# A backward kernel for an S4 layer gated by a SwiGLU: stores of the gate gradients by quarters, and a pause in the parameter chunks

## The chip, the cores and the metric

The kernel runs on 1 core of one Trainium2 chip. The metric is the time of one execution on the device in microseconds (us). The engines are named as in the profile: PE is TensorE (matmul), DVE is VectorE, ACT is ScalarE, POOL is GpSimd, SP is SyncE. All engines run side by side, each through a queue of its own in a fixed order. DMAs are issued from such a queue too (here those of SP, POOL and ACT), so a transfer that stands behind a waiting instruction is issued late.

## The reference

With L = 2048 tokens, D = 576 channels, N = 128 states and F = 4608 hidden units, the forward pass is, cut to what matters:

```python
xn = layernorm(x)
s  = irfft(rfft(xn) * rfft(K)) + xn * Dskip      # K from A, B, C, log_dt: an S4 convolution along L
h  = silu(xn @ w1) * (xn @ w3)                   # SwiGLU: w1, w3 are D x F
g  = silu(h @ w2)                                # w2 is F x D
out = x + s * g
```

The kernel returns `out` (out_0) and, for a given `grad_out`, the gradients of x (out_1), of A, B and C (real and imaginary parts), log_dt (out_8), Dskip, w1 (out_10), w3 (out_11) and w2 (out_12). Inputs and outputs are bfloat16.

## The kernel before

**Stages.** The forward part (layernorm, the convolution as a transform by matmuls, the SwiGLU) fills about the first 800 us. It leaves the gate products in device memory: `G_dram` holds xn @ w1 and `U_dram` xn @ w3, in NG = 18 groups of FG = 256 hidden units. Everything after that is in `backward`, which lays three streams of work over each other:

1. The **gradient pass**, 18 groups, to 1705 us in the profiled execution. `phase6_load` brings a group's G and U on POOL's queue into `gg_n` and `h_n` (L1192, L1193, 1 MB each); ACT makes Silu into `gu_n` (L1197) and then Derivative_silu in place (L1199); DVE multiplies both with U (L1201, L1202). There are two sets of these three buffers, so group gi+1 is loaded and prepared while group gi is worked on, and its load must wait until the buffers of group gi-1 are free. `phase6_group` then makes the gradient of the hidden units. In four steps s, each for two token tiles in both halves j of the sequence, PE computes `ph` from `goT` and `w2T` (L1224), ACT copies it to `gh` (L1227), and DVE multiplies `gh` into `gu_n` and `gg_n` (L1230). After the second and the fourth step PE computes half of the gradient of w2 (`phase6_grad2`, matmuls L1251, eviction `gw2` L1255, store to out_12 on POOL L1256). After all four steps POOL stores `gu_n` and `gg_n` as GU and GG in device memory, `GU_dram` and `GG_dram`, in two halves of 512 KB each (L1233 to L1236). Last, `phase6_grad13` computes the gradients of w3 and w1 (matmuls `pgw` L1270, evictions `gw` L1272).

2. The **parameter chunks** of the convolution, 36 of them (`ssm_bwd_params`). For each, `param_load` issues on SP two small loads `gz` (L1007), a transposing DMA `qT` from `Q_dram`, and a load `pz` (L1012); three chunks' buffers exist, and loads run two chunks ahead. `param_chunk` does 16 matmuls into `et_ps` in four quads (L1025), and after each quad DVE makes two products `pr_q` (L1032) and a sum into `S_all` (L1036). When all chunks are done, `phase5_final` closes this work in five pieces of up to 128 channels: PE transposes `S_all` (L1055), ACT copies it to `ST`, DVE does some 45 small operations per piece with the rates loaded by `load_rates`, and each piece's results `gout` go out through three buffers on SP and ACT. A last small store, `gl_bf` to out_8, is issued on SP (L1118, L1120).

3. The **second pass** (`phase6_inputs`), from 1705 us on: the gradient of xn for 16 tiles of 128 tokens. Each tile needs `ggc` and `guc`, transposing DMAs of GG and GU on SP (`nat_transpose`, L1177), then 144 matmuls `px` of 128x288 (L1314) against the transposed weights. `finish` adds the convolution's part (`gx`, DVE L1324), and `ln_bwd_tile` goes back through the layernorm and stores out_1. `ggc`, `guc` and the two `px` each have two buffers, so a tile may begin when the tile two before it has let go of them. The 36 blocks of the transposed weights come in four parts (blocks 0 to 15, 16 to 22, 23 to 29, 30 to 35), brought by SP as well: `wTA` in good time during the gradient pass; part 1 and half of part 2 into the gradient pass's buffers once they are free (the profile calls them `gg_n`, `h_n` and `gu_n` there too); the other half of part 2 (`wTB`) and part 3 (`wT`) when their space is free. Because the weights come one after another, the first two tiles are computed part by part, both tiles in each part.

**The order.** A scheduler builds each engine's queue when the program is built. `self.at(us)` gives the instructions that follow a due time, which serves as their priority: of those that are ready in the scheduler's model, the one due first goes first. On the chip each queue then runs in the order so fixed. The call is `backward(700, TG=36, TQ=75, TC=14, TX=18)`: in due times, the gradient pass starts at T0 = 700 with a group each 36; the chunks start at T1 = 1000, one each 14; the second pass starts at T2 = 700 + 18 x 36 = 1348, a tile each 18. Due times are not device times, only their order counts.

Of the kernel before, what the change touches and what calls it, by code (L numbers as in the profile page):

```python
# [60 lines left out]
class K:  # L61
# [837 lines left out]
            for g in range(4):  # L899
                self.conv_bwd_quarter(g, kp, zp, ps, T0 + g * TQ, TQ)  # L900

    def ssm_bwd_params(self, T0, TC, S_all, ps):
        cfg = self.cfg
        D, LT = cfg.D, cfg.LT
        with self.tc.tile_pool(name="g_k", bufs=1, side="right") as gkp, self.tc.tile_pool(name="g_q", bufs=2, side="right") as qp:
            gz = []
            for i in range(3):
                z = gkp.tile([P, 2, 2, 2, 16, LT], BF16, name=f"gz{i}")
                self.nc.gpsimd.memset(z[:], 0.0)
                gz.append(z)  # L910
            NCH = D // 16
            AHEAD = 2
            q = []
            for ch in range(NCH + AHEAD):
                if ch < NCH:
                    self.at(T0 + TC * (ch - AHEAD))
                    q.append(self.param_load(ch, gz[ch % 3], qp))
                if ch >= AHEAD:
                    self.at(T0 + TC * (ch - AHEAD))
                    self.param_chunk(ch - AHEAD, q.pop(0), S_all, qp, ps)  # L920

    def conv_bwd_quarter(self, g, kp, zp, ps, T0, TQ):
# [202 lines left out]
    def backward(self, T0, TG, TQ, TC, TX, gctx, mats):  # L1125
        nc, cfg = self.nc, self.cfg
        D, L, LT, F, FT = cfg.D, cfg.L, cfg.LT, cfg.F, cfg.FT
        self.GG_dram = self.dram.tile([LT, P, F], BF16, name="GG_dram")
        self.GU_dram = self.dram.tile([LT, P, F], BF16, name="GU_dram")
        self.GXN_dram = self.dram.tile([P, LT, D], FP32, name="GXN_dram")  # L1130
        NG = F // self.FG
        T2 = T0 + TG * NG
        FA = 16
        pool = self.tc.tile_pool
        PS = bass.MemoryType.PSUM
        with ExitStack() as out:
            ffn = ExitStack()
            wp = ffn.enter_context(pool(name="e_w", bufs=2))
            inp = [self.in0, ffn.enter_context(pool(name="e_in1", bufs=1))]
            elp = ffn.enter_context(pool(name="e_el", bufs=3))  # L1140
            gwp = ffn.enter_context(pool(name="e_gw", bufs=2))
            ps_h = ffn.enter_context(pool(name="e_ps_h", bufs=3, space=PS))
            ps_gw = ffn.enter_context(pool(name="e_ps_gw", bufs=2, space=PS))
            ps = out.enter_context(pool(name="b_ps", bufs=3, space=PS, side="right"))
            self.ssm_bwd_conv(T0, TQ, ps)
            mats.close()
            fix = out.enter_context(pool(name="b_fix", bufs=1, side="right"))
            S_all = fix.tile([P, 4, D], FP32, name="S_all")
            wA = out.enter_context(pool(name="x_wA", bufs=1, side="right"))
            wT = [[self.load_wT1(wA.tile([P, FA, D], BF16, name=f"wTA{k}"), k, 0, FA, T2 - 190 + 75 * k, 15) for k in range(2)]]  # L1150
            T1 = T0 + 4 * TQ
            self.ssm_bwd_params(T1, TC, S_all, ps)
            self.at(T1 + TC * D // 16)
            self.phase5_final(out, fix, S_all, ps, T1 + TC * D // 16, TX)
            cur = self.phase6_load(0, T0 - TG, TG, wp, inp)
            for gi in range(NG):
                nxt = self.phase6_load(gi + 1, T0 + TG * gi, TG, wp, inp) if gi + 1 < NG else None
                self.at(T0 + TG * gi)
                self.phase6_group(gi, cur, elp, gwp, ps_h, ps_gw)
                cur = nxt  # L1160
            ffn.close()
            gctx.close()
            self.phase6_inputs(T2, TX, FA, wT)
# [15 lines left out]
    def phase6_load(self, gi, T, TG, wp, inp):  # L1179
        nc, cfg = self.nc, self.cfg  # L1180
        self.at(T)
        D, DT, LT = cfg.D, cfg.DT, cfg.LT
        aps = self.aps
        FG = self.FG
        assert 2 * (DT * P - D) == P
        w2T = wp.tile([P, DT, FG], BF16, name="w2T")
        self.nat_transpose(w2T[:], self.W2_dram[gi * FG:(gi + 1) * FG, :])
        inp = inp[gi % 2]
        gg = inp.tile([P, LT, FG], BF16, name="gg_n")
        hn = inp.tile([P, LT, FG], BF16, name="h_n")  # L1190
        gu = inp.tile([P, LT, FG], BF16, name="gu_n")
        nc.gpsimd.dma_start(out=gg[:], in_=self.G_dram[gi])  # L1192
        nc.gpsimd.dma_start(out=hn[:], in_=self.U_dram[gi])  # L1193
        quarters = [slice(s * LT // 4, (s + 1) * LT // 4) for s in range(4)]
        self.at(T + 0.4 * TG)
        for sl in quarters:
            nc.scalar.activation(out=gu[:, sl, :], in_=gg[:, sl, :], func=ACT.Silu)  # L1197
        for sl in quarters:
            nc.scalar.activation(out=gg[:, sl, :], in_=gg[:, sl, :], func=ACT.Derivative_silu)  # L1199
        for sl in quarters:  # L1200
            nc.vector.tensor_tensor(out=gg[:, sl, :], in0=gg[:, sl, :], in1=hn[:, sl, :], op=ALU.mult)  # L1201
            nc.vector.tensor_tensor(out=hn[:, sl, :], in0=gu[:, sl, :], in1=hn[:, sl, :], op=ALU.mult)  # L1202
        return w2T, hn, gg, gu

    def phase6_group(self, gi, tiles, elp, gwp, ps_h, ps_gw):
        nc, cfg = self.nc, self.cfg
        D, LT, FG = cfg.D, cfg.LT, self.FG
        nfull = D // P
        rem = D - nfull * P
        LH = LT // 2  # L1210
        w2T, hn, gg, gu = tiles
        pair = lambda t_: t_[:].rearrange("p (j t) f -> p j t f", j=2)
        for s in range(LH // 2):
            gh = elp.tile([P, 2, 2, FG], BF16, name="gh6")
            ph = [ps_h.tile([P, 2, FG], FP32, name="ph") for _ in range(2)]
            for k in range(2):
                t = s * 2 + k
                for j in range(2):
                    tt = j * LH + t
                    rs = slice(j * rem, (j + 1) * rem)  # L1220
                    steps = [(self.goT[:, c, tt * P:(tt + 1) * P], w2T[:, c, :]) for c in range(nfull)]
                    steps.insert(nfull * (1 - j), (self.goTt[rs, t * P:(t + 1) * P], w2T[rs, nfull, :]))
                    for n, (lw, rh) in enumerate(steps):
                        nc.tensor.matmul(ph[j][:, k, :], lhsT=lw, rhs=rh, start=(n == 0),  # L1224
                                         stop=(n == nfull))
            for j in range(2):
                nc.scalar.copy(out=gh[:, j], in_=ph[j][:])  # L1227
            sl = slice(s * 2, s * 2 + 2)
            for t_ in (gu, gg):
                nc.vector.tensor_tensor(out=pair(t_)[:, :, sl], in0=gh[:], in1=pair(t_)[:, :, sl], op=ALU.mult)  # L1230
            if s % 2 == 1:
                self.phase6_grad2(gi, s // 2, hn, gwp, ps_gw)
        for (dst, t_) in ((self.GU_dram, gu), (self.GG_dram, gg)):  # L1233
            for j in range(2):
                ts = slice(j * LH, (j + 1) * LH)
                nc.gpsimd.dma_start(out=dst[ts, :, gi * FG:(gi + 1) * FG].rearrange("t p f -> p t f"), in_=t_[:, ts, :])  # L1236
        self.phase6_grad13(gi, gg, gu, gwp, ps_gw)

    def phase6_grad2(self, gi, fl, hn, gwp, ps_gw):
# [239 lines left out]
```

## Time and profile before

| | us |
|---|---|
| five runs | 2050.97, 2033.35, 2070.73, 2043.77, 2058.24 |
| their median | 2050.97 |
| the profiled execution | 2074.11 |
| span in its profile, first to last instruction | 2072.3 |

| engine | busy us | share of the span |
|---|---|---|
| PE (16144 instructions) | 1788.5 | 86% |
| DVE | 1505.3 | 73% |
| ACT | 968.4 | 47% |
| POOL | 468.2 | 23% |

The core's DMA engines moved 421.27 MB, 203 GB/s on average. The mean granted clock of PE was 0.95 of full speed. L12 is line 12 of the kernel's file. In a row of the timeline the columns are: start, duration, engine (SPq is SP's queue, where DMAs are issued), line, operation, output<-input, shapes, and in brackets the idle time before it with what ended it.

### The profile page before, as it was taken

How to read it: one execution, taken by the hardware profiler on the slowest of the kernel's cores; microseconds unless marked ns; L12 is line 12 of the kernel's file. 1: busy time of each engine (PE TensorE's matmuls, PEld its weight loads, DVE VectorE, ACT ScalarE, POOL GpSimd, SP SyncE). 2: the span in 40 equal slices, each digit the busy share in tenths (PEclk: the TensorE clock that was granted, in tenths of full speed). 3: DMA queues.
4: the chain of work that ended last, by engine and by line, in shares of the span. 5: the costliest groups of instructions: out<-in, count | busy, mean ns of one | idle time of the engine just before them, and what ended most of it. 6: DMA issues, size and time to landing. Idle time of an engine off the chain costs nothing. (4 is left out here: it accounts for less than half of the span.)

```text
span 2072.3 us, 40290 instructions
## 1 busy us (share of the span) xinstructions
PE 1788.5 (86%) x16144; PEld 1250.7 (60%) x16214; DVE 1505.3 (73%) x2616; ACT 968.4 (47%) x1733; POOL 468.2 (23%) x610
## 2 busy tenths in 40 slices
PE   2888988889898799989898999876996994899997
PEld 1443333335453577777777777755775773677785
DVE  7459999998783465478696878666895985677851
ACT  1968888886455311474747565333453420000000
POOL 6016666661123011111111111211211210000000
PEclk9899999999999899999999999988998997899998
DMA  6688788877579988546463635999878799999894
GB/s 177 238 278 294 265 279 276 283 259 253 177 260 191 213 202 190 170 134 190 130 196 117 205 126 160 202 224 172 241 204 152 209 234 180 219 230 191 171 176 62
DMA packets 550828, 421.27 MB, mean 203 GB/s; under 512 B 414320, under 2 KB 481072, under 8 KB 546032
## 3 DMA queue, kind: packets, MB, share of 16 engines
q1 hardware_dynamic: 488096, 254.56, 52.0%
q0 software_dynamic: 37904, 147.48, 22.6%
q10 hardware_dynamic: 24640, 16.65, 3.0%
q8 instruction: 127, 2.08, 0.4%
q14 instruction: 61, 0.50, 0.1%
HBM read 135.96 MB, written 196.27 MB: 160 GB/s over the span
## 5 line engine op out<-in xcount | busy, mean ns | idle before, releaser
L1270 PEld LDWEIGHTS <-xn_bf 128*128 128x128 bf16 x2304 | 225.1, 98 | 30.1 <-issue 2.6
L1032 DVE TENSOR_TENSOR pr_q<-et_ps,pz 128x512 f32<-128x512 f32 x288 | 186.1, 684 | 68.4 <-DMA pz<-PZ_dram 32.3
L768 PEld LDWEIGHTS <-xnT 128*128 128x128 bf16 x1152 | 101.7, 98 | 172.6 <-issue 76.5
L1224 PE MATMUL ph<-w2T,goT 128*128 128x256 bf16 x1152 | 179.2, 287 | 3.4 <-DVE e L840 2.0
L1036 DVE TENSOR_REDUCE S_all<-pr_q 128x16 f32<-128x1024 f32 x144 | 175.0, 1216 | 2.2
L1251 PE MATMUL pgw<-go_o,h_n 128*128 128x288 bf16 x1152 | 163.8, 292 | 0.0
L768 PE MATMUL pu<-wmB_w,xnT 128*128 128x512 bf16 x565 | 152.9, 386 | 5.0 <-ACT u_t L778 3.7
L768 PE MATMUL pg<-wmB_w,xnT 128*128 128x512 bf16 x523 | 145.6, 382 | 9.1 <-issue 5.6
L499 POOL COPY pz_k<-p_k 128x256 bf16<-128x256 bf16 x144 | 140.2, 1016 | 46.5 <-issue 37.4
L1272 ACT CAST gw<-pgw 128x256 bf16<-128x256 f32 x144 | 54.6, 380 | 204.0 <-PE pgw L1270 202.7
L831 PE MATMUL po<-w2g,hc 128*128 128x288 bf16 x1152 | 147.5, 291 | 1.3 <-ACT u_t L778 1.3
L1363 ACT ACTIVATE t<-gx 128x576 f32<-128x576 f32 x16 | 10.9, 684 | 282.1 <-DVE gx L1324 282.1
L1314 PEld LDWEIGHTS <-guc 128*128 128x128 bf16 x1152 | 114.4, 100 | 44.8 <-DMA guc<-GU_dram 14.9
L1314 PEld LDWEIGHTS <-ggc 128*128 128x128 bf16 x1152 | 114.5, 100 | 39.1 <-DMA ggc<-GG_dram 9.4
L1230 DVE TENSOR_TENSOR gu_n<-gh,gu_n 128x1024 bf16<-128x1024 bf16 x72 | 49.4, 686 | 120.8 <-ACT gh L1227 120.8
L1270 PE MATMUL pgw<-gu_n,xn_bf 128*128 128x256 bf16 x1152 | 132.8, 272 | 1.5 <-ACT gw L1255 1.1
L831 PEld LDWEIGHTS <-hc 128*128 128x128 bf16 x1152 | 113.2, 99 | 32.5 <-issue 1.7
L1270 PE MATMUL pgw<-gg_n,xn_bf 128*128 128x256 bf16 x1152 | 130.8, 274 | 0.0
L1025 PE MATMUL et_ps<-gz,qT 128*128 128x128 bf16 x576 | 53.9, 228 | 89.0 <-DMA qT<-Q_dram 53.0
L1224 PEld LDWEIGHTS <-goT 128*128 128x128 bf16 x1152 | 103.2, 102 | 45.5 <-issue 14.2
L1251 PEld LDWEIGHTS <-h_n 128*128 128x128 bf16 x1152 | 112.7, 100 | 28.7
L1314 PE MATMUL px<-wTA,guc 128*128 128x288 bf16 x512 | 109.5, 297 | 13.1 <-DMA guc<-GU_dram 13.1
(321 smaller groups left out, 4232.3 us busy)
## 6 DMA issues: line engine op xcount, KB each, us to landing
G_dram<-g_t POOLq DMA_DIRECT2D x72, 256.0 KB, 3.9
U_dram<-u_t POOLq DMA_DIRECT2D x72, 256.0 KB, 3.3
H_dram<-h_t SPq DMA_DIRECT2D x72, 256.0 KB, 3.2
Q_dram<-q_k SPq DMA_DIRECT2D x36, 512.0 KB, 3.5
gg_n<-G_dram POOLq DMA_DIRECT2D x18, 1024.0 KB, 5.6
h_n<-U_dram POOLq DMA_DIRECT2D x18, 1024.0 KB, 8.9
GU_dram<-gu_n POOLq DMA_DIRECT2D x36, 512.0 KB, 6.3
GG_dram<-gg_n POOLq DMA_DIRECT2D x36, 512.0 KB, 8.5
```

The costliest lines, as they stand in the source:

```text
L499: nc.gpsimd.tensor_copy(out=pz[:, g, h, 1:3], in_=pv[:, g, h])
L768: nc.tensor.matmul(pt[:], lhsT=xnT[:, c, ts], rhs=wm[w][:, c, :], start=(c == 0 and not first), stop=(c == nfull - 1 and first))
L831: nc.tensor.matmul(po_[:, pi_, 0:pw], lhsT=hc[:, fi, :], rhs=w2[fi][:, po:po + pw], start=(fi == 0), stop=(fi == FT - 1))
L1025: nc.tensor.matmul(T[h][:, :, dd].rearrange("p r k (f t) -> p r (k f) t", f=2), lhsT=qT[:, dl, :], rhs=gK[:, :, :, :, dl, :].rearrange("p ...
L1032: nc.vector.tensor_tensor(out=pr[:, r].rearrange("p k m a -> p m k a"), in0=T[h][:, r][:, None].to_broadcast([P, 2, 4, 2, AV]), in1=pz[:, ...
L1036: nc.vector.tensor_reduce(out=S_all[:, :, d0:d0 + 4].rearrange("p (s k) d -> p k s d", k=2), in_=pr[:].rearrange("p r k (s d) a -> p k s d ...
L1224: nc.tensor.matmul(ph[j][:, k, :], lhsT=lw, rhs=rh, start=(n == 0), stop=(n == nfull))
L1230: nc.vector.tensor_tensor(out=pair(t_)[:, :, sl], in0=gh[:], in1=pair(t_)[:, :, sl], op=ALU.mult)
L1251: nc.tensor.matmul(pgw[pi_][:, 0:pw], lhsT=hn[:, tt, fl * P:(fl + 1) * P], rhs=go_o[:, tt, po:po + pw], start=(tt == 0), stop=(tt == LT - 1))
L1270: nc.tensor.matmul(pw_[:, 0:FG], lhsT=self.xn_bf[:, tt, c * P:(c + 1) * P], rhs=nat[:, tt, :], start=(tt == 0), stop=(tt == LT - 1))
L1272: nc.scalar.copy(out=gw[:, c, :], in_=pw_[:, 0:FG])
L1314: nc.tensor.matmul(px[pi_][:, 0:pw], lhsT=act[:, fi, :], rhs=wT[p][ai][:, fi - f0, po:po + pw], start=(fi == 0 and ai == 0), stop=(fi == F ...
```

## The change

Three edits. First, in `phase6_group` the stores of GU and GG go inside the loop over s: after the second and the fourth step, the token tiles finished so far are stored, two halves j of each array, before the w2 gradient of that step. That makes eight stores of 256 KB per group where there were four of 512 KB. Second, in `phase6_load` the due time of Silu and what follows goes from 0.4 to 0.45 of a group's 36. Third, in `ssm_bwd_params` a chunk whose due time lies after T2 - 30 = 1318 gets 40 more; with 1000 + 14c that is chunk 23 and all after it. The due times of `phase5_final` are not changed.

```diff
-    def ssm_bwd_params(self, T0, TC, S_all, ps):
+    def ssm_bwd_params(self, T0, TC, T2, S_all, ps):
...
             NCH = D // 16
             AHEAD = 2
             q = []
+            when = lambda c: T0 + TC * c + (40 if T0 + TC * c > T2 - 30 else 0)
             for ch in range(NCH + AHEAD):
                 if ch < NCH:
-                    self.at(T0 + TC * (ch - AHEAD))
+                    self.at(when(ch - AHEAD))
                     q.append(self.param_load(ch, gz[ch % 3], qp))
                 if ch >= AHEAD:
-                    self.at(T0 + TC * (ch - AHEAD))
+                    self.at(when(ch - AHEAD))
                     self.param_chunk(ch - AHEAD, q.pop(0), S_all, qp, ps)
...
-            self.ssm_bwd_params(T1, TC, S_all, ps)
+            self.ssm_bwd_params(T1, TC, T2, S_all, ps)
...
         quarters = [slice(s * LT // 4, (s + 1) * LT // 4) for s in range(4)]
-        self.at(T + 0.4 * TG)
+        self.at(T + 0.45 * TG)
...
             if s % 2 == 1:
+                for (dst, t_) in ((self.GU_dram, gu), (self.GG_dram, gg)):
+                    for j in range(2):
+                        ts = slice(j * LH + 2 * s - 2, j * LH + 2 * s + 2)
+                        nc.gpsimd.dma_start(out=dst[ts, :, gi * FG:(gi + 1) * FG].rearrange("t p f -> p t f"),
+                                            in_=t_[:, ts, :])
                 self.phase6_grad2(gi, s // 2, hn, gwp, ps_gw)
-        for (dst, t_) in ((self.GU_dram, gu), (self.GG_dram, gg)):
-            for j in range(2):
-                ts = slice(j * LH, (j + 1) * LH)
-                nc.gpsimd.dma_start(out=dst[ts, :, gi * FG:(gi + 1) * FG].rearrange("t p f -> p t f"), in_=t_[:, ts, :])
         self.phase6_grad13(gi, gg, gu, gwp, ps_gw)
```

## The prediction

> **What bounds the kernel now.** First the slices of the page: busy tenths of TensorE (PE) and of the DMA engines over the span, about 52 us each.
>
> ```profile
> PE   2888988889898799989898999876996994899997
> ...
> DMA  6688788877579988546463635999878799999894
> ```
>
> PE is the bound wherever it shows 8 or 9. Counted from 0, it drops in slices 26, 27, 30 (the gradient pass) and 33 (the start of the second pass), with the DMA row at 7 to 9: these stalls the change can reach. What ends them is in the table of waits (waiter <- releaser: total us, times, longest).
>
> ```profile
> ACT  L1197 <- DMA gg_n<-G_dram: 57.3, 7, 18.6
> PE et_ps L1025 <- DMA qT<-Q_dram: 53.0, 3, 27.5
> POOL gg_n L1192 <- DMA GG_dram<-gg_n: 25.9, 2, 17.8
> ```
>
> Read upwards: POOL may not reload gg_n before the store of its old contents has landed (8.1 and 17.8 us late in two groups); ScalarE (ACT) waits for that load in its Silu, with the eviction gh queued behind it; PE waits for gh. In the worse case PE stood 16.8 us, at 1585 to 1602. In between, the longest single stall is a parameter chunk's qT. PE's timeline at the start of the second pass, and SP's:
>
> ```profile
> 1730.98 0.39 PE L1025 MATMUL et_ps<-gz,qT 128*128 128x128 bf16 x4
> ...
> 1761.24 0.61 PE L1025 MATMUL et_ps<-gz,qT 128*128 128x128 bf16 x4 [27.55 <-DMA qT<-Q_dram]
> ```
> ```profile
> 1727.05 7.82 SPq L1177 DMA_TRANSPOSE wTB<-in_B_w_dram  x5
> ...
> 1736.31 13.54 SPq L1177 DMA_TRANSPOSE wT<-in_B_w_dram  x10
> ...
> 1756.49 2.27 SPq L1177 DMA_TRANSPOSE qT<-Q_dram  x1
> ```
>
> SP issues without a gap from 1668 to 1759. A chunk stands before the tiles' products in PE's queue, and its qT behind all weight transposes in SP's. Last, the end of the span, from the chain that ended last:
>
> ```profile
> 2000.74 34.70 PE px L1314 x284
> 2035.45 9.60 DMA guc<-GU_dram
> 2045.09 20.05 PE px L1314 x141
> ```
> and SP before it:
> ```profile
> 2013.66 1.31 SPq L1118 DMA_DIRECT2D out_dram<-gl_bf  x1
> ...
> 2018.17 17.19 SPq L1177 DMA_TRANSPOSE ggc<-GG_dram  x1
> 2035.45 6.67 SPq L1177 DMA_TRANSPOSE guc<-GU_dram  x1
> ```
>
> The small store of gl_bf (512 elements of 2 bytes) took 18.1 us to land, and the transpose behind it ran 17.19 us instead of its usual 4.6: the last tile lost 9.6 us.
>
> **Part 1, stores by halves of a group.** Four stores of 512 KB become eight of 256 KB, half of them issued after the second of four ph steps. POOL: the old issue took 0.9 us; at that price for the half-size one too, at most 4 x 0.9 = 3.6 us more per group of about 37, on an engine busy 23%; its long waits (for ACT and DVE) take it. h_n's load and the 144 KB store of out_12 now stand behind stores that wait for DVE's products; h_n is needed a group later, so this costs nothing; without that cover, some us per group. The Trainium skill ("DMA: Bandwidth & Descriptors", section Bandwidth) speaks against it: batch DMAs to 1 MiB or more; its section Anatomy of one DMA puts a fixed 2.0 us on each. By that rule 4 x 18 x 2.0 = 144 us more if nothing overlapped. The row stands against it: POOL issues the four stores at 0.9 us apart and they land 6.3 to 8.5 us later, so the fixed parts overlap; the trace's issue price, hidden, gives 0. I take 0.
>
> The gain: in the group of the 16.8 us stall the queue held h_n (1 MB), then 2 MB of stores, and the last GG store landed 28.5 us after its issue. Half of that now goes out about 10 us earlier (DMA was about half busy there), so 3 MB become 2 and landing may come some 10 us sooner: 16.8 becomes about 7. The other late store (8.1 us) is partly covered by a qT wait of 8.3 us. The third stall, 17.1 us at 1409 to 1426, comes from a gg_n load that itself took 24 us; it stays. Ends: 0 (the same bytes jam elsewhere) and 25 (both late stores cured). I take **-8**, below the middle, because the profiled run is 23 us slower than the median and may hold more such jams.
>
> **Part 2, Silu due at 0.45 instead of 0.40.** The order of instructions of the two programs shows ACT's queue in the pass unchanged but for one gw eviction, DVE's in one group, PE's by a few matmuls. 0.
>
> **Part 3, chunks of 23 and up due 40 us later.** In PE's new order the opening tiles 0 and 1 run parts 0, 1 and 2 with only 16 chunk matmuls between, then 12 of the next chunk, then part 3. In SP's new order all ggc and guc pieces come first, then gz, wTB, wT, and only then qT. From the old durations: SP reaches the first ggc at 1698 as before (the qT ahead of it still ends there); ggc, pz, guc, ggc, guc 14, twelve short transposes of 1.33 with gaps 16, gz 1.2, wTB 7.8, wT 13.6: 1751. Then qT 2.3, landing 4.7 after issue: 1756. PE does parts 0 and 1 until about 1732, waits for wTB until 1740, does part 2 until 1747, and waits for that qT until 1756. So the stall isn't gone, it is 8 + 9 instead of 27. DVE's pair for the chunk (2.58 us) holds part 3 a little: tile 0 ends at 1763. Tile 2's transposes may start then (its buffers are tile 0's), and guc landed 12.7 us after the start of ggc in the old trace, with one pz between; say 12.2: tile 2 starts at 1775 instead of 1789.6. **-14**.
>
> Three chunks more are now left for the loop (155 matmul quarters of four after tile 2 starts, against 108). Old tiles with chunks took 18.7 to 20.8 us, tiles 9 and 10 without 18.1. With the old cadence (tiles 2 and 3 40 in all, 4 to 10 20.8, 18.7, 19.2, 19.6, 19.2, 19.3, 19.3) tile 11 starts at 1951.4 instead of 1964.6: **-13** of the 14 is left.
>
> **The tail.** The closing parameter work (phase5_final, five pieces) was one piece per tile, from tile 9 on. In the new order all of it is later, bunched: four of the five PE transposes fall in tile 11, and in DVE's queue pieces 0, 1 and 2 stand before the gx additions of tile 11. Those free px, and px has two buffers: tile 13 can't begin before them. Count from the start of tile 11: last chunk's DVE 4 x 2.58 and tile 10's closing 3.9 with starting gap, 14.8; then the rate loads, whose space is the chunks', 9.3 (1931.9 to 1941.2 in the old trace); then the three pieces, 133 rows of about 0.2 (the 128x1 ones 0.07), 22.5; waits for the three gout buffers about 5 (old: 17.8 over five pieces). Sum 51.6. Old: tile 13 at 2000.7 - 1964.6 = 36.1 after tile 11. So 16 later. After such a stall PE restarts slow (PEclk 0.74 around the old last stall, and the last tile took 20.05 for 17.6): 2 more. Then gl_bf becomes ready near 77 and stands between ggc and guc of the last tile: guc lands about 26.7 after gl_bf's issue (2013.7 to 2040.4, when the old ggc landed), 32 after tile 13's end instead of 27: 5 more. **+23**. If gout stores are cheap and the loads take 7: +8; if each piece takes 13 and guc lands later still: +33.
>
> **Sum.** -8 - 13 + 23 = +2 on the profiled execution's 2074.1 us. That execution stands above all five runs shown (2033.4 to 2070.7, median 2051.0); carried to the median: 2053.
>
> **Rivals.**
> 1. Faster. The early stores cure both late landings and the opening gains its full 16 with a short tail (DVE done early, guc not held): -25 - 14 + 8 = -31, about 2020; partly cured, about 2026. For it: the 25.9 us row. Against: bunched DVE rows in one queue, which no earlier store shortens.
> 2. Slower. DVE's queue at tile 11 decides the end: the stores cure nothing, the opening saves 8, the tail costs 33: +25, 2076. It decides once the DVE part exceeds 51.6 by about 10, that is, with gout landings near the 10 us they had at the end of the old trace rather than their median of 2.5.
> 3. The pause doesn't do what it says, because 12 chunk matmuls still stand before part 3 behind a late qT: opening gain near 0, other terms as taken: +15, 2066, within 1%.
>
> **Chances.** No difference beyond 1% (about what a measurement of this kernel can tell from no change), my case and rival 3: 0.45. Faster by more (rival 1): 0.25. Slower by more (rival 2, and rival 3 with a longer tail): 0.30. My case's own range is 2035 to 2070; with the ends of both open terms the range is 2026 to 2080.
>
> **What would show it.** Right: the 27.5 us qT wait falls under 12, tile 2's first px comes near 1775 (from the same start of the span), the wait POOL gg_n <- GG_dram shrinks, px of tile 13 starts over 45 us after tile 11's, a long guc transpose behind gl_bf ends the chain. Wrong: tile 13 without a stall (then rival 1), a gradient pass as long as before or longer, POOL waits that hold gg_n.

## The result, and the profile after

| | median us | runs | lowest to highest |
|---|---|---|---|
| before | 2064.32 | 79 | 2029.68 to 2107.81 |
| changed | 2047.96 | 44 | 2027.77 to 2081.68 |

The ratio of changed to before is 0.9991, 95% interval 0.9970 to 1.0011: no difference that this comparison can tell. It leaves out runs over 1.5% above the fastest of their kernel, and since the times of the changed kernel spread over 2.7% and those of before over 3.9%, that cuts both to much the same band; over all runs the medians lie 0.8% apart. Run beside each other on one chip (e3_after, below), the ratio was 0.9952 (0.9913 to 0.9991). So the change brings between nothing and 1%.

The profiled execution took 2060.61 us (span 2058.8) against 2074.11 before: 13.5 less. The page's slices:

```profile
PE   2888989989899599989998999897996995999985
...
DMA  6678778877579998536463645999889899999974
```

Slice 33, the opening of the second pass, is 5 where it was 4; the last slice is 5 where it was 7; slices 26 and 27, in the gradient pass, are 9 and 7 where they were 7 and 6. The table of waits, in the rows that answer to those of before (waiter <- releaser: total us, times, longest):

```profile
PE et_ps L1026 <- DVE pr_q L1033: 25.4, 7, 16.6
...
ACT L1198 <- DMA gg_n<-G_dram: 17.1, 1, 17.1
...
POOL gg_n L1193 <- DMA GG_dram<-gg_n: 15.9, 1, 15.9
...
PE et_ps L1026 <- DMA qT<-Q_dram: 14.5, 2, 13.6
```

PE's wait for qT falls from 53.0 to 14.5 us. But POOL still waits 15.9 us for one store of GG, and PE's longest wait (16.6 us, through DVE) is still there. PE at the opening, then the chain that ended last:

```profile
1714.58 0.40 PE L1316 MATMUL px<-wTB,guc 128*128 128x288 bf16 x1 [6.21 <-DMA wTB<-in_B_w_dram]
...
1750.76 0.66 PE L1316 MATMUL px<-wTA,ggc 128*128 128x288 bf16 x2 [12.13 <-DMA ggc<-GG_dram]
```
```profile
1961.40 4.59 DMA out_dram<-gout
1978.05 32.25 PE px L1316 x247
2010.30 21.65 DMA guc<-GU_dram
2032.00 19.62 PE px L1316 x141
```

The one stall of 27.55 us is gone from the opening; what is late next is the weights (6.2 us) and tile 2's own ggc (12.1). At the end the last guc takes 21.65 us where it took 9.60 in the chain before.

To compare kernels I cut each profile at two points: the first chunk's matmul (near 1310 us in all) and the end of the last pgw matmul, where the gradient pass ends. The first part had no such difference between before and after (the first chunk starts at 1316.1 and 1318.2). **The stretch** between the points, and the second pass behind it to PE's end:

| | stretch | second pass | sum |
|---|---|---|---|
| before | 389.0 | 360.1 | 749.1 |
| changed | 366.3 | 367.2 | 733.5 |

The stretch gave 22.7 us, the second pass took back 7.1; with a start 2.0 us later, PE ends 13.5 us sooner. These are one execution of each kernel.

### The profile page after: what moved, and what is told of

Same layout as the page of the kernel before. It is cut to its first block, busy times and chain, and to the rows that moved or that the text cites. A ratio compares the mean times of both kernels' runs of the same rounds, so it can differ in the third digit from the quotient of the medians.

```text
span 2058.8 us, 40441 instructions
## 1 busy us (share of the span) xinstructions
PE 1785.8 (87%) x16144; PEld 1246.6 (61%) x16214; DVE 1502.1 (73%) x2616; ACT 968.3 (47%) x1733; POOL 514.1 (25%) x682
## 5 line engine op out<-in xcount | busy, mean ns | idle before, releaser
L1316 PE MATMUL px<-wTA,ggc 128*128 128x288 bf16 x512 | 110.6, 297 | 17.8 <-DMA ggc<-GG_dram 12.1
L1228 ACT CAST gh<-ph 128x512 bf16<-128x512 f32 x144 | 82.6, 606 | 83.3 <-PE ph L1225 52.8
```

Source lines behind the costliest of these rows:

```text
L1316: nc.tensor.matmul(px[pi_][:, 0:pw], lhsT=act[:, fi, :], rhs=wT[p][ai][:, fi - f0, po:po + pw], start=(fi == 0 and ai == 0), stop=(fi == F ...
```

## The experiments

Ratios are to the kernel before, run beside it on the same chip, with 95% intervals. "Late landings" counts the places in the stretch where a load or a store of POOL's queue landed more than 17 us after its issue.

| label | what | ratio | stretch | second pass | late landings |
|---|---|---|---|---|---|
| e1_stores | half-group stores alone | 0.9897 (0.9837 to 0.9957) | 369.5 | 367.2 | 2 |
| e2_pause | pause alone | 0.9998 (0.9945 to 1.0051) | 389.3 | 371.3 | 3 |
| e3_after | changed kernel again | 0.9952 (0.9913 to 0.9991) | 363.9 | 369.4 | 2 |
| e4_gl_act | changed, gl_bf on ACT | 0.9890 (0.9838 to 0.9941) | 362.0 | 364.1 | 1 |
| e5_gl_rows | changed, gl_bf in rows | 0.9892 (0.9843 to 0.9941) | 377.0 | 359.1 | 2 |
| e6_small_late | 8 small stores, written after the fourth step | 0.9903 (0.9871 to 0.9935) | 354.0 | 359.6 | 1 |
| e7_gg_first | GG stored before GU | 1.0044 (1.0006 to 1.0083) | 377.0 | 367.5 | 2 |
| e8_stores_tc13 | e1, chunks each 13 | 0.9957 (0.9924 to 0.9989) | 357.7 | 367.6 | 1 |
| e9_loads4 | e6, both loads in 4 | 0.9874 (0.9811 to 0.9937) | 355.0 | 370.1 | 0 |
| e10_stores16 | 16 stores of 128 KB | 1.0010 (0.9934 to 1.0086) | 391.2 | 363.7 | 3 |
| e11_half_parts | 8 stores by half partitions | 1.0077 (1.0013 to 1.0141) | 426.0 | 368.8 | 4 |
| e12_small_gl | e6, gl_bf in rows | 0.9831 (0.9777 to 0.9885) | 357.8 | 347.9 | 1 |
| e12b_small_gl | the same on another chip | 0.9810 (0.9745 to 0.9875) | 374.8 | 348.1 | 2 |
| e13_hn4 | e12, h_n in 4 pieces | 0.9730 (0.9668 to 0.9792) | 350.3 | 360.4 | 1 |
| e14_small_gl_pause | e12 with the pause | 0.9782 (0.9722 to 0.9842) | 380.2 | 355.9 | 2 |
| e15_hn4_pause | e13 with the pause | 0.9838 (0.9770 to 0.9907) | 339.5 | 359.2 | 0 |
| e16_hn4_only | before, h_n in 4 pieces | 0.9888 (0.9846 to 0.9929) | 359.8 | 365.5 | 1 |
| e18_early_qt | e12, one chunk's loads early | 0.9843 (0.9781 to 0.9905) | 365.5 | 349.4 | 1 |

Before itself has 3 late landings, the changed kernel 2. A stretch is one execution and moves among like kernels by up to 17 us (e12 and e12b are the same program); the groups of like kernels are what is compared.

### The parts of the change

e1_stores has the diff's stores and nothing else of it; PE's, DVE's and ACT's queues keep the order of before, and SP's but for one place (below). e2_pause has the two `when` calls and nothing else.

> The kernel before with the stores of GU and GG by halves of a group, and nothing else. If the stores are what shortened the gradient pass (1705.2 to 1684.5 us at its end in the two profiles), the pass ends near 1685, the second pass keeps the 360 us of before, and the time is 15 to 20 us under before: ratio about 0.992. The prediction's own term is -8: ratio 0.996. If the shorter pass was one execution's luck, the stores are worth 0: pass end near 1705, ratio 1.000. In each case the 26 us landing of the stores at the group near 1560 tells whether fewer bytes in the queue help: the prediction said it falls to some 18.

> The kernel before with the pause of 40 in the chunks' due times alone; stores by whole groups and Silu at 0.40 as before. If the profiles' sum holds, the pass ends near 1705 as before, tile 2 starts about 13 us earlier in the second pass, the end 7 us later: second pass 367 against 360, ratio 1.003. The prediction had +10 here, ratio 1.005. If the pause also frees the pass (fewer qT in it), the pass ends at 1690 or before, and this kernel alone shows the gain: ratio 0.995 or less.

The stores alone gain 1.0% and take 20 us off the stretch; the pause alone leaves the stretch at 389.3 and the ratio at 1. So the gain is that of the edit of the stores, and it lies in the gradient pass: the second pass was 367.2 us in e1, no shorter than in before. But the landing near 1560 did not fall: at 1528 in e1_stores the second half's GG stores landed 27.8 us after their issue, with half the bytes of the group already gone.

> The changed kernel once more, unedited, on the same chip as the others of this group. From the profiles so far: the stores take 20 us off the stretch from the first chunk to the end of the gradient pass (389 us with the old stores, 362 to 377 with the new), the pause adds 0 to 8 us to the second pass. So this kernel is expected 10 to 20 us under before, ratio 0.990 to 0.995. If stores and pause together do nothing, it stays at 1.000.

0.9952, a hair above the expected 0.990 to 0.995. Its stretch was 363.9 us, its second pass 369.4.

### Early, small, or first?

e6_small_late writes eight stores of four token tiles each, after the fourth step; e7_gg_first only swaps the two arrays; e10 and e11 vary the pieces, also written after the fourth step (e10 two tiles per store, e11 eight tiles from half of the partitions). The diffs are cut:

```diff
e6   -            for j in range(2):
     -                ts = slice(j * LH, (j + 1) * LH)
     +            for j in range(4):
     +                ts = slice(j * LH // 2, (j + 1) * LH // 2)
e7   -        for (dst, t_) in ((self.GU_dram, gu), (self.GG_dram, gg)):
     +        for (dst, t_) in ((self.GG_dram, gg), (self.GU_dram, gu)):
e10  +            for j in range(8):
     +                ts = slice(j * LH // 4, (j + 1) * LH // 4)
e11  +                for h in (slice(0, P // 2), slice(P // 2, P)):
```

> The kernel before with eight stores of 256 KB per group instead of four of 512 KB, but all after the fourth step, as the four were. If it is the early issue of the first half that shortens the pass, nothing changes: first chunk to end of pass 389 us, ratio 1.000. If it is the size of the single transfer (smaller ones mix better with the transposes), the stretch falls to about 370 and the ratio to 0.990.

> The kernel before with GG stored ahead of GU, nothing split and nothing earlier. POOL reloads gg_n only when GG's store has landed, so if that wait is what the new stores shorten, GG landing a half of the stores earlier should bring part of the gain: stretch 375 to 383, ratio 0.993 to 0.997. If the gain comes from fewer bytes beside the transposes at the end of a group, whichever array they belong to, nothing changes: 389 and 1.000.

e6 gains as much as e1 (0.9903 against 0.9897). But its stores are late only in the program's text. A store of four token tiles needs only its own tiles finished, and in the queue that the scheduler built half of the stores stand behind the second step, ahead of h_n's load, as in e1. POOL in e6:

```profile
1516.22 1.52 POOL L1236 DMA_DIRECT2D GU_dram<-gu_n  x2 [10.36 <-DVE gu_n L1230]
...
1518.52 1.49 POOL L1236 DMA_DIRECT2D GG_dram<-gg_n  x2
1527.05 0.55 POOL L1193 DMA_DIRECT2D h_n<-U_dram  x1 [7.03 <-PE pgw L1251]
...
1528.23 1.51 POOL L1236 DMA_DIRECT2D GU_dram<-gu_n  x2
1529.73 1.49 POOL L1236 DMA_DIRECT2D GG_dram<-gg_n  x2
```

In before all four stores of this group go out within 2.7 us, behind h_n. So e6 does not part early from small, and the early issue stays a possible cause. e7 gains nothing (1.0044), so landing GG ahead of GU is not enough. The page's list of issues for before and for e6 (output<-input, count, KB each, median us to landing) shows what the smaller stores do at the median:

```profile
GU_dram<-gu_n POOLq DMA_DIRECT2D x72, 256.0 KB, 4.0
GG_dram<-gg_n POOLq DMA_DIRECT2D x72, 256.0 KB, 5.3
```

Before, x36 of 512 KB landed in 6.3 and 8.5 us. The smaller ones land about 3 us sooner, which by itself PE would not see.

> Sixteen stores of 128 KB per group after the fourth step (packets of 1 KB). If smaller is better without end, the stretch falls below the 354 us of eight stores and the ratio below 0.990. If the fixed part of each DMA begins to count, the last GG store lands later, the stretch grows again to 375 or more and the ratio goes to 0.995 or above.

> Eight stores of 256 KB per group after the fourth step, but each from half of the partitions: the size of a transfer is halved as in the eight small stores, the size of a packet (one partition's eight tiles, 4 KB) is not. If the packet's size is what counts, this is as before: stretch 377 to 389 us, ratio 1.000. If the transfer's size or the number of transfers counts, it gains like the eight small stores: 354 to 370, ratio 0.990.

Neither gains. In e11 one transfer is as small as in e6, but each needs all four steps; from 1400 on its stores stand behind h_n's load, as in before, and the stretch is 426 us. That speaks for the early issue and against the size alone. e10 is no clean test: at least half of its sixteen stores go out early, but the scheduler also changed the order of PE's queue (in 18 places) and of DVE's, ACT's and SP's.

A third difference goes with the shape of the stores. In every kernel with four tiles per store SP sends the second chunk's qT and pz ahead of its two gz (in e1 qT at 1300.7, gz from 1306.9); in before, e2, e7, e11 and e16 the gz go first (in before gz from 1314.5, qT at 1315.6). No run has one without the other. So the edit of the stores gains 1%; whether by the early issue, the size or this swap on SP the runs do not settle.

My reading before these runs, that the packet's size decides, fails too: the DMA records of the traces show packets of 4096 bytes for the stores of every one of these kernels (of 8192 for the load of h_n), so halving or quartering a store changed no packet. What goes with the time is the count of late landings: 2 to 4 in the kernels with eight tiles per store and h_n whole, 1 or 2 in the eleven with four tiles per store and h_n whole, 3 with two tiles.

### The stall that stays

In the changed kernel's trace POOL's queue, and SP's, near 1540:

```profile
1537.81 0.55 POOL L1194 DMA_DIRECT2D h_n<-U_dram  x1 [6.79 <-PE pgw L1253]
1538.35 1.52 POOL L1236 DMA_DIRECT2D GU_dram<-gu_n  x2
1539.87 1.49 POOL L1236 DMA_DIRECT2D GG_dram<-gg_n  x2
...
1569.35 0.55 POOL L1193 DMA_DIRECT2D gg_n<-G_dram  x1 [15.89 <-DMA GG_dram<-gg_n]
```
```profile
1537.21 6.95 SPq L1178 DMA_TRANSPOSE qT<-Q_dram  x1
```

A qT goes out 0.6 us ahead of h_n's 1 MB. The 26 us from 1538 on, by the page of that window (each figure is 0.65 us; a packet's time and bytes are booked where it starts):

```profile
DMA  7679944543987997987889999699919929299999
GB/s 202 163 89 250 71 40 28 42 47 45 137 173 191 215 205 214 221 200 227 211 240 282 225 145 157 98 121 90 115 68 90 94 58 97 35 312 377 362 183 151
```
```profile
h_n<-U_dram POOLq DMA_DIRECT2D x1, 1024.0 KB, 26.7
GU_dram<-gu_n POOLq DMA_DIRECT2D x2, 256.0 KB, 27.3
GG_dram<-gg_n POOLq DMA_DIRECT2D x2, 256.0 KB, 28.0
...
qT<-Q_dram SPq DMA_TRANSPOSE x2, 21.9
```

All of them land together, 22 to 28 us after their issue, and gg_n's reload stands behind GG. Little is moved from 1541.2 to 1544.5 (28 to 47 GB/s) and from 1553.6 to 1560.8 (35 to 157); in between it is 137 to 282. The lower DMA share at 1541 to 1544 is only the booking: by the packet records twelve packets of 8192 bytes of POOL's loads were then in flight, for 4.1 to 7.5 us each, where such a packet takes 0.31 us at the median.

This stall is not in every execution. In e3_after, the same program on another chip, the qT went out as close (0.60 us ahead, at 1544), h_n landed after 13.8 us and PE did not stall there; its late landings, of 17 to 20 us, came at 1408 and 1494. The same place shows in before (1558) and in e1, e2, e4, e5, e6, e7, e11 and e12, each time with qT 0.4 to 0.6 us ahead of h_n. e8_stores_tc13 moved the chunks against the groups:

```diff
-        k.backward(700, 36, 75, 14, 18, gctx, mats)
+        k.backward(700, 36, 75, 13, 18, gctx, mats)
```

> The stores by halves, and the chunks due each 13 instead of 14, without the pause. Two chunks fewer are left for the second pass, whose early tiles with chunks took 18.7 to 20.8 us against 18.1 without: 2 to 6 us less there. The chunks' qT also stand elsewhere among the groups. In all six profiles so far one qT is issued about 0.6 us ahead of the load of h_n near 1530 to 1560; both then land 21 to 30 us later and PE stands 13 to 18 us. If this meeting of the two is the cause, the stall goes or moves to another group, and the time may fall by up to 16 us against stores alone; if the cause is that group's own addresses, it stays at the same group.

The late landing at 1525 is gone and one at 1464 has come (qT 24.7, gg_n 20.6 us; PE 16.05 us at 1489). There the qT went out 4.5 us ahead of the load of gg_n. So it is a meeting of transfers, not that group's data. The two chunks fewer in the second pass brought nothing: 367.6 us.

e9_loads4 cuts both loads of 1 MB into four, e13_hn4 and e16_hn4_only that of h_n alone (their diff, cut):

```diff
-        nc.gpsimd.dma_start(out=hn[:], in_=self.U_dram[gi])
+        for sl in quarters:
+            nc.gpsimd.dma_start(out=hn[:, sl, :], in_=self.U_dram[gi][:, sl, :])
```

> Eight stores of 256 KB after the fourth step, and besides the loads of gg_n and h_n in four pieces of 256 KB each instead of one of 1 MB. In the jams of the traces POOL's packets of 8 KB and 4 KB take up to 7 us each while the transposes beside them crawl. If it is the large packets that meet the transposes badly, loads with packets of 2 KB shrink the last jam too: the PE stall of 13 to 18 us falls under 6, the stretch from first chunk to end of pass from 354-370 to about 345, ratio 0.983. If only stores matter, 0.990 as with small stores alone. If each DMA has its price on POOL, eight more per group make it slower: 0.995 or above.

> The same with the load of h_n in four pieces of 256 KB (packets of 2 KB); every other queue keeps its order. If h_n's 8 KB packets are what meets the qT near 1530 to 1560, the PE stall there (11.7 to 13.3 us with small stores) falls under 5 and the ratio lies about 0.005 below the reference of this group. If not, the stall stays, and three DMAs more per group cost 0 to 3 us.

> The kernel before with the load of h_n in four pieces and nothing else: stores of 512 KB as before. If large packets of any kind beside a qT make the jam, the stall near 1560 to 1600 shrinks but does not go, and the one near 1430 stays: stretch from first chunk to end of pass 370 to 380 against 389, ratio 0.992 to 0.996. If h_n alone is the partner, it goes: stretch 355 to 365, ratio 0.985 to 0.988. If the stores are, 389 and 1.000.

In e9, e13, e15 and e16 PE's stall near 1560 is gone altogether. e13's two waits for qT (39.4 us) are elsewhere, at 1404 and at the opening. Its POOL queue at the same meeting, with a qT issued at 1531.20:

```profile
1531.80 0.56 POOL L1196 DMA_DIRECT2D h_n<-U_dram  x1 [6.77 <-PE pgw L1253]
...
1532.95 1.51 POOL L1238 DMA_DIRECT2D GU_dram<-gu_n  x2
1534.45 1.65 POOL L1238 DMA_DIRECT2D GG_dram<-gg_n  x2
1536.09 1.10 POOL L1196 DMA_DIRECT2D h_n<-U_dram  x2
1543.27 0.54 POOL L1196 DMA_DIRECT2D h_n<-U_dram  x1 [6.08 <-DMA h_n<-U_dram]
...
1548.43 0.55 POOL L1193 DMA_DIRECT2D gg_n<-G_dram  x1 [0.98 <-PE et_ps L1025]
```

The meeting still happens, and GG still lands some 12 us after its issue, but that is soon enough: gg_n's reload goes out at 1548 with no wait for it. e16 is the cleanest pair of all, since PE's, DVE's, ACT's and SP's queues keep the order of before. It shows that h_n is enough for this place (0.9888 by itself, a stretch of 359.8 us), but not for the others: with the old stores PE still lost 13.55 us to a qT at 1407, in the time of the weight transposes. e13, with both, has the lowest ratio measured, 2.7% under before (0.9668 to 0.9792); its interval overlaps that of e12b (0.981), which lacks only the cut of h_n. e9's second cut, of gg_n, let the scheduler reorder PE's queue; its first chunk came at 1333.8 us, later than in any other, so its ratio says little on gg_n.

Two things differ in e13 at once. The longest packet on POOL's queue fell from 7 to 8 us (before, changed, e6) to 3.5, since h_n's packets went from 8192 to 4096 bytes; and only 256 KB of h_n, not 1 MB, now stand ahead of the GG store. The Trainium skill ("DMA: Bandwidth & Descriptors", section Queues, rings and completion order) says that each DMA engine takes turns between queues a whole packet at a time, which would speak for the packets; no run here shows it, and the runs do not separate the two.

### The tail and the opening

e4_gl_act issues gl_bf's store with `nc.scalar` instead of `nc.sync`. e5_gl_rows turns it first:

```diff
+            glT = ps2.tile([P, 4, N], FP32, name="et_ps")
+            nc.tensor.transpose(glT[0:DT, 0, :], glogdt[:], self.ident_f[:])
+            gl_bf = big.tile([P, P], BF16, name="gl_bf")
+            nc.vector.tensor_copy(out=gl_bf[0:DT], in_=glT[0:DT, 0, :])
...
+                nc.sync.dma_start(out=aps["out_8"][0:nfull * P].rearrange("(c p) -> c p", p=P), in_=gl_bf[0:nfull, :])
```

> The changed kernel with the small stores of gl_bf issued on ACT's queue instead of SP's. If the last tile's guc is late because it stands behind gl_bf in SP's queue, it is issued at once, takes its usual 5 us, and the last stall of 16.4 us shrinks to about 5: the time falls by about 10 us against the changed kernel. If the store's 2-byte pieces hold up the DMA engines wherever they come from, the guc that runs beside it still takes 15 us or more and the time stays.

> The changed kernel with gl_bf turned by one PE transpose first, so that it goes out in 5 rows of up to 256 bytes instead of 576 pieces of 2 bytes; issued on SP as before. Both theories of the last stall give about -10 us against the changed kernel: the guc behind it takes 5 us. If this one gains and the store on ACT's queue does not, it is the small pieces; if both gain, the queue; if neither, the long guc has another cause.

> Eight small stores after the fourth step and gl_bf turned to rows by a PE transpose before it goes out; no pause. Without the pause the last tile lost 9.6 us to the transpose behind gl_bf in the first profile, 4 to 5 in others. Expected: second pass 3 to 6 us under the 360 to 367 of the kernels without the pause, ratio 0.988. If gl_bf costs nothing when it comes early, as here, 0.990.

e4 is neither of the two cases expected. On ACT's queue the store went out at 1994.09 and landed 16.2 us later. ggc, issued on SP 3 us before it, landed only with it (19.6 us), and the last guc, which waited for ggc's landing, went out at 2010.72; PE's waits for the two were 11.8 us, where the changed kernel had 16.4 for guc. So it is not only the place in SP's queue: the store of 512 pieces of 2 bytes takes 16 to 18 us from either queue, and a transpose near it is late. In rows the guc behind it takes 5.25 us, and the chain of e12 ends without a wait:

```profile
1974.19 46.07 PE px L1315 x376
```

The second pass falls to 347.9 and 348.1 us without the pause, and to 359.1 with it. The ratios of e12 and e12b (0.983 and 0.981) lie under e6's.

> Eight small stores after the fourth step and gl_bf in rows, unedited, as the reference of this group: ratio 0.983 again, within 0.978 to 0.989.

> The reference of this group with the pause of 40. If the pause costs by the chunks that it leaves for the end (DVE's bunched closing work before tile 13, and the last tiles), the opening gains about 11 us, the end loses 17 to 20: second pass 354 to 358 against 348, ratio 0.003 to 0.005 above the reference. If its only cost was the store of gl_bf ahead of the last guc, it is now 5 to 10 us faster than the reference.

> Eight small stores after the fourth step, h_n in four pieces, gl_bf in rows, and the pause of 40. Without the pause this kernel had ratio 0.973. The second pass took 355.9 us with the pause and 348 without in two profiles of the kernels without h_n's pieces, so 0.975 to 0.978 is expected; if the pause is worth its opening (11 us) instead, 0.968.

The pause in the second pass, by the profiles: with gl_bf as it was, 367.2, 369.4 and 371.3 us with the pause against 359.6 to 370.1 without (eight kernels with a chunk each 14, mean 365.3); with rows, 355.9, 359.1 and 359.2 against 347.9, 348.1, 349.4 and 360.4. The first two groups overlap. In the second the cure of gl_bf has a price of its own: its PE transpose stands in PE's queue ahead of the last tile, and with the pause PE waits there 5.4 to 5.9 us for DVE (e5, e14, e15; without the pause 0.8 to 0.9). In e14:

```profile
2014.13 0.37 PE L1114 MATMUL et_ps<-ident_f,glogdt 128*5 128x128 f32 x1 [5.43 <-DVE glogdt L1097]
```

Both ends of the pause show in every profile: with it (seven kernels) tile 2's first guc product comes 68.7 to 75.0 us after the pass and tile 13 starts 44.2 to 45.2 us after tile 11; without it and with a chunk each 14 (twelve kernels) 80.1 to 90.9 and 36.2 to 38.3. So it gains some 13 us at the opening and loses some 8 before tile 13; what it costs in all depends on the last tile and is not shown. Nor do the times show a cost: e2 has 0.9998; e14 was expected 0.003 to 0.005 above e12b and lies 0.003 below it, with wide overlap; e15 missed its 0.975 to 0.978 with 0.9838, but e13 and e15 were on two chips. Whether the pause is worth a loss of 0.3% or nothing stays open.

e18_early_qt moved one chunk's loads ahead of the weights on SP, with all other queues in the order of e12:

```diff
+                    due = T0 + TC * (ch - AHEAD)
+                    self.at(T2 - 16 if T2 - 16 < due < T2 else due)
```

> The reference of this group with the loads of chunk 26 due just ahead of the second pass's own loads instead of behind them: its gz, qT and pz then stand on SP ahead of wTB and wT, and no other queue changes its order. If the opening stall of 28 us is only that qT, PE goes on to the next late thing (part 2 and part 3 of the weights): the stall shrinks to some 13 us in pieces, tile 2 starts about 14 us sooner, and as no chunk is moved the end follows in full: second pass 334 to 338 against 348, ratio 0.006 below the reference. If the weights behind it are as late as the qT was, the gain is under 4 us.

Missed. PE's 28.7 us in one piece became four smaller ones:

```profile
1704.69 0.61 PE L1026 MATMUL et_ps<-gz,qT 128*128 128x128 bf16 x4 [6.46 <-DVE S_all L1037]
...
1723.23 0.66 PE L1316 MATMUL px<-wT,ggc 128*128 128x288 bf16 x2 [5.27 <-DMA ggc<-GG_dram]
...
1731.29 0.50 PE L1026 MATMUL et_ps<-gz,qT 128*128 128x128 bf16 x3 [6.30 <-DMA qT<-Q_dram]
...
1749.15 0.66 PE L1316 MATMUL px<-wTA,ggc 128*128 128x288 bf16 x2 [9.51 <-DMA ggc<-GG_dram]
```

and tile 2 started 76.5 us after the pass, as in e12 (77.3). DVE (the chunk's products), then part 3's ggc, the next qT and tile 2's ggc were each late in turn. The first qT was only the last of several things that come through SP one after another.

## Why the prediction was right or wrong

The likeliest outcome, no difference beyond 1%, came, and 2047.96 lies in the range; but the sum that led there was +2 us on the profiled execution where -13.5 came, and beside before on one chip the changed kernel was 0.5% faster (e3_after). That the median lies in the range is partly luck: the range was built on the five-run median of 2050.97, and over 79 runs that of before is 2064.32. The step that failed is Part 1.

**Part 1, the stores: the term was mis-sized, and the gain lay elsewhere.** It took -8: half the bytes go out earlier, so the late GG store lands 10 us sooner and the stall of 16.8 us becomes 7. That stall stayed (16.56 us in the changed kernel, 11.7 to 21.4 in the other kernels with whole h_n loads that had it in one piece): with half of the stores already gone the last GG store still landed 28.2 us after its issue, where it was 28.8. The gain came in the stretch before it: the stalls of 8.3, 5.4 and 17.1 us between 1350 and 1426, 30.8 together, became 3.0 and 13.55. The step had the 17.1 stay, which it nearly did (13.55, again behind a gg_n load that took 19 us beside a qT), and the other late store, in whose group the 8.3 fell, it counted for little. The term measured -22.7 in this pair, and over all the stretch was 354 to 380 us in eleven kernels with such stores, 377 to 389 in three with the old ones. Its model was bytes over bandwidth; in the jam 28 to 47 GB/s were moved for over 3 us and some 90 for seven more, against 219 on average from 1300 to 1684, so the bytes left to move did not set the time. Why the stores' edit gains is open: early issue, size and the swap on SP go together in every kernel that gained by it. The cost side held: eight issues cost nothing that shows. The rule of 1 MiB and more (the Trainium skill, "DMA: Bandwidth & Descriptors", section Bandwidth), set aside by the issue row, would have misled further: cutting h_n's load of 1 MB in four took 1.1% off by itself (e16).

**Part 2: not tested.** No run has the 0.45 alone.

**Part 3, the opening: right.** Tile 2 was to start 14 us earlier after the pass; by its first guc it did by 13.5 (70.9 us after the end of the pass against 84.4). The pieces differ: 9.8 us went to the weights where I had 8, the chunk's qT then cost nothing, and tile 2's ggc took 12.1. "13 of the 14 is left at tile 11" was 10.1. The sum agrees better than its terms, which is in part luck; that the opening gains shows in all seven kernels with the pause.

**The tail: right in kind, too long.** Tile 13 began 44.4 us after tile 11, not 51.6 (old 36.2): 8 us later where I had 16. The terms: the last chunks 12.8 us for 14.8, the wait for the rates 5.0 for 9.3, the pieces with their waits for gout 26.4 for 27.5. From tile 13 to the end 9.0 us more where I had 7: guc behind gl_bf as foretold, and PE slow after it (19.6 us for the last tile). The second pass as a whole came out 7.1 us longer; the prediction's -13 + 23 was +10. But e1, without the pause, had the same 367.2 us, so one pair does not show that the pause makes the pass longer as a whole; the later tile 13 shows in all seven kernels with it.

Of the rivals, the third (the pause does nothing at the opening) and the second (DVE decides by 10 us more) fell; the first had the sign of the stores' gain, but only one of the two late stores was cured, and its short tail did not come.

## What to carry to other kernels

When a transfer lands late, look at what the DMA engines moved in that window before dividing bytes by bandwidth. Here busy engines with a fifth or less of the usual GB/s meant a meeting of a transposing DMA with large loads and stores, and cutting one load of 1 MB into four took the stall away and 1.1% off (e16), while having half of the stores gone beforehand left it as it was (16.56 us). Before an experiment is read, look at the order that the scheduler built: e6, written late, stored early. A gain at the opening of a stage that only moves work to its end is given back there at least in part (13 us against 8 and the last tile's waits); count the engine that must do the moved work. And store a column vector as rows: 512 pieces of 2 bytes took 16 to 18 us, and the transpose near them was late.

## What the runs showed of the hardware

- The stores' packets were 4096 bytes whether a store was 512, 256 or 128 KB: cutting these transfers did not cut their packets. Cutting h_n's load did (8192 to 4096).
- How close a load stood behind a qT told how late it landed. Over all twenty traces 27 loads of 1 MB were issued 0.4 to 1.0 us after a qT, and they took 13.4 to 30.7 us to land; the 17 issued 1.0 to 1.2 us after one took 7.1 to 12.4. Where the load was cut in four, seven pieces that stood as close took 6.4 to 11.7. Some loads further behind a qT were late too (23.6 us at 1.6 us in before), so closeness is not the only way into a jam.
- After a stall PE runs slow for some microseconds, as the prediction took it. In e1_stores, after 6 us of idle at 1858 to 1864, the granted clock was 0.50 from 1864 to 1868 (1.00 before the stall, from 1850 to 1857):

```profile
1866.67 0.69 PE L1315 MATMUL px<-wTA,guc 128*128 128x288 bf16 x2
...
1868.53 0.41 PE L1315 MATMUL px<-wTA,ggc 128*128 128x288 bf16 x2
```

The same pair of matmuls takes 0.69 us until 1867 and 0.41 us from 1868 on, so this stall cost about 2 us beyond its own length, an estimate from 4 us at half the pace.
